# Two rows of scores in one burst, one shared bank for keys, queries and outputs, and a new order of steps in a fused attention, experts and gated-layer kernel

## The chip, the cores and the metric

The kernel runs on one core of a Trainium2 chip. The metric is the device time of one execution in microseconds (us), lower is better. One launch holds the whole computation.

## The reference, cut to what matters

Three layers follow one another, all in float32. The attention has 4 batches of 12 heads with 448 positions and a head width of 64:

```python
scores = scale * np.matmul(q_n, k_n.transpose(0, 1, 3, 2))   # q_n, k_n: rms-normed
scores = scores - np.max(scores, axis=-1, keepdims=True)
attn = np.exp(scores)
attn = attn / (np.sum(attn, axis=-1, keepdims=True) + 1e-09)
return np.matmul(attn, v).astype(np.float32)
```

Its output, 1792 tokens of width 768, goes through 8 experts, one per token:

```python
expert_idx = np.argmax(logits, axis=1)
...
    h = np.maximum(x[mask] @ w1[e], 0.0)
    out[mask] = gate_w[mask, None] * (h @ w2[e])
```

and then through a gated layer: `(gate * val @ w_out)` with `gate = 1 / (1 + exp(-(x @ w_gate)))` and `val = x @ w_val`.

## The kernel before, in words

**Tiling.** The 48 heads are worked through as 24 pairs (G = 2). The 448 query positions of a head are R = 4 "rows" of P = 112 positions. For one row of a pair, `scores` (L338) issues six products of 448 columns: three steps (high times high, high times low, low times high) for each of the two heads. A head takes only 64 of TensorE's 128 rows, so the two heads of a step use the two halves of the array. The result of a head and a row fills one PSUM bank. `peaks` (L351, VectorE) takes the maximum, `exps` (L359, ScalarE) the exponential, and with it the bank is free. `turn_p` (L382, TensorE) transposes 112 columns of all four rows into a bank, `high_p` (L391, ScalarE) and `low_p` (L401, VectorE) split it into a rounded and a rest part, and `values` (L411, TensorE) multiplies both with the values, two products each. After four of them `copy_o` (L425, ScalarE) moves the result to memory, `outputs` (L432, TensorE, eight products) turns it back to positions, and `weigh` (L441, VectorE) divides by the sums. Keys and queries of the next pair come by `turn_k` and `turn_q` (transposes, L313 and L327), `high_k` and `copy_q` (ScalarE, L316 and L330) and `low_k` (VectorE, L320); TensorE turns what `scale_k`, `scale_q`, `high_q` and `low_q` on GpSimd and ScalarE have prepared. `turn_q` is done twice per pair, for the high and for the low part.

**Banks.** PSUM has eight banks here, in four pools: `pss` with 3 (scores), `pst` with 2 (turned probabilities), `psx` with 2 (turned keys and queries, outputs, ranks, and later the turned tokens of the experts) and `psv` with 1 (values). A pool hands its banks out in turn, and whoever gets a bank waits until its last reader is done.

**Order.** Every step of the attention stage is put into one list with a place (a number; one row of a pair is 1, so a pair is 8), and the list is sorted by place (`todo`, L645 to L778). Each engine runs its own instructions in the order in which the sorted list issues them, so a step that waits holds up all that stands behind it on its engine. `WITHIN` (L122) gives the places of a pair's steps relative to its start, `PLACE` (L115) those of the preparation and the routing, `FIRST`, `SECOND` and `EARLY` (L135, L121 and L145) those of the first pairs, and `LT` (L113) moves the last batch's routing. At the end of each batch the routing of its tokens runs beside the attention of the next: `sum_squares` on ScalarE, `choice`, `norms`, `ranks` (three small products into a `psx` bank, L570), `places` and `gates` on VectorE and GpSimd, and `send`, an indirect DMA from GpSimd.

**Experts.** `experts` (L1179) goes through the experts, expert 0 in `first_expert`, then e = 1 to 7 in the loop at L1280. Its second half is a loop over o, six blocks of 128 output columns. At each o, `window_turn(e + 1, o)` (L1198) transposes one block of the next expert's tokens into a `psx` bank, and `high_low` (L1162) reads it, first on ScalarE, then on VectorE. Then come the products of block o, the copy of their result, and `advance` (L1396), the splitting of weights, also on ScalarE and VectorE. From expert 5 on the outputs are taken in pairs (`paired`, L1027): both products of o = 0 and o = 1 are issued at o = 0, none at o = 1, so that the `window_turn` of o = 2 follows directly on that of o = 1:

```python
                if e + 1 < E:
                    window_turn(e + 1, o)
...
                if o == 0 or not paired(e):
                    outs = [result_ps(e) for i in range(2 if paired(e) else 1)]
...
                elif o > 1:
```

**Banks after the attention.** `gemm_ps` (L1034) takes `pss` and `pst` in turn, `either_ps` (L1041) goes through the list `BANKS` (L1039).

## Time and profile before

| | us |
|---|---|
| median of 3 runs | 1170.42 (1170.27 to 1172.71) |
| the profiled execution, its own time | 1169.98 |
| its span, first to last instruction | 1168.3 |
| TensorE products busy in the span | 1135.9 (97%) |
| TensorE weight loads busy | 1020.8 (87%) |
| VectorE busy | 848.0 (73%) |
| ScalarE busy | 568.4 (49%) |
| GpSimd busy | 304.1 (26%) |

How to read it: the span is that of the profiled execution; what lies around it is 1.7 us. PE is TensorE's products, PEld its weight loads, DVE is VectorE, ACT ScalarE, POOL GpSimd. Products are pipelined and their ends are modelled, so the start of one to the start of the next says what a group of products takes, not the length of one. The attention stage ends some 355 us after the span's start, the experts take it to about 650 us, and the gated layer follows.

### The profile page before, as it was taken

Reading aid. Unit: us, or ns where it says so; the run is one execution under the profiler, and the core shown is the slowest. Engines: PE = TensorE matmul, PEld = TensorE weight load, DVE = VectorE, ACT = ScalarE, POOL = GpSimd, SP = SyncE. Lnnn points to the kernel's source line nnn. Section 1 sums busy time; section 2 is a strip of 40 time slices with the busy share of each in tenths; the row PEclk is TensorE's granted clock in tenths of the full one; section 3 lists DMA queues with packets and bytes.
Section 4 is the critical chain, followed back from the end, with each engine's and each line's share of the span. In section 5 each row is a group of like instructions: output and inputs, shape, how many; then the busy total and the mean of one; then the engine's idle time right before and its main releaser. Section 6 shows DMA issues by size and latency. Waiting matters only on the chain.

```text
span 1168.3 us, 19626 instructions
## 1 busy us (share of the span) xinstructions
PE 1135.9 (97%) x7294; PEld 1020.8 (87%) x7295; DVE 848.0 (73%) x1615; ACT 568.4 (49%) x1281; POOL 304.1 (26%) x490
## 2 busy tenths in 40 slices
PE   4999999999999999999999999999999999999996
PEld 2777777777779999999999999999999999999996
DVE  5898899898873155566677968878888868336663
ACT  6789988989872153565666512122211212332220
POOL 5765768778731000000000000000000000021132
PEclk9999999999999999999999999999999999999998
DMA  4414813221235354566767134443444433832031
GB/s 110 127 33 123 259 49 95 49 49 49 73 127 178 110 176 157 180 218 198 224 214 216 55 109 135 153 146 122 152 132 136 132 125 107 345 133 85 27 129 55
DMA packets 97944, 154.55 MB, mean 132 GB/s; under 512 B 4891, under 2 KB 82459, under 8 KB 96947
## 3 DMA queue, kind: packets, MB, share of 16 engines
q1 hardware_dynamic: 91119, 125.69, 34.9%
q0 software_dynamic: 6432, 27.53, 6.3%
q8 instruction: 58, 0.95, 0.3%
q14 instruction: 43, 0.35, 0.1%
q10 hardware_dynamic: 292, 0.03, 0.0%
HBM read 117.84 MB, written 35.39 MB: 131 GB/s over the span
## 4 chain that ended last, share of the span: by engine, by line
PE 63%; issue 3%; POOL 1%; DMA 1%; POOLq 0%
PE psg L1170 42%; PE pso L1170 8%; PE psg L1174 5%; PE psg L1177 2%; PE psg L898 2%; POOL out_dram L797 1%; PE psg L894 1%; PE psw L1205 1%; DMA wout<-wod 1%; PE psw L865 0%; POOL dummy L804 0%; PE pso L1148 0%; POOLq L1817 0%; POOLq L797 0%
## 5 line engine op out<-in xcount | busy, mean ns | idle before, releaser
L1170 PE MATMUL psg<-xs,w 128*128 128x448 f32 x1728 | 351.3, 365 | 0.0
L1170 PEld LDWEIGHTS psg<-xs,w 128*128 128x128 f32 x1728 | 323.9, 188 | 27.1
L1465 POOL DMA_DIRECT2D wod<-so x42 | 22.8, 542 | 601.7 <-DVE hA L1607 352.1
L1170 PE MATMUL pso<-wout,hs 128*128 128x384 f32 x882 | 153.4, 335 | 0.4 <-DMA wout<-wod 0.4
L1170 PEld LDWEIGHTS pso<-wout,hs 128*128 128x128 f32 x882 | 153.0, 188 | 0.7 <-issue 0.6
L1021 DVE TENSOR_TENSOR whl<-raw,whl 128x768 fp32r<-128x768 f32 (+1 forms) x98 | 105.1, 1072 | 60.2 <-ACT whl L1017 60.0
L353 DVE TENSOR_REDUCE nm<-pss 112x1 f32<-112x448 f32 x192 | 116.6, 618 | 26.2 <-PE pss L346 25.4
L406 DVE TENSOR_TENSOR pl<-pst,ph 112x448 fp32r<-112x448 f32 x192 | 115.7, 616 | 17.7 <-ACT ph L393 15.9
L369 ACT ACTIVATE pn<-pss,nm 112x448 f32<-112x448 f32 x184 | 119.2, 648 | 6.7 <-DVE nm L353 6.4
L393 ACT CAST ph<-pst 112x448 fp32r<-112x448 f32 x192 | 101.7, 539 | 21.2 <-PE pst L386 18.5
L386 PE MATMUL pst<-ident,pn 112*112 112x112 f32 x768 | 107.2, 267 | 2.4 <-DVE pl L406 2.3
L386 PEld LDWEIGHTS pst<-ident,pn 112*112 112x112 f32 x768 | 79.0, 136 | 29.1 <-DVE pl L406 12.3
L346 PE MATMUL pss<-kh,qt 64*112 64x448 f32 x384 | 86.8, 425 | 4.1 <-ACT pn L369 3.0
L1017 ACT CAST whl<-raw 128x768 fp32r<-128x768 f32 (+1 forms) x98 | 90.7, 926 | 0.0
L420 PE MATMUL psv<-ph,vt 112*128 112x448 f32 x192 | 82.5, 430 | 0.0
L1443 ACT CAST w<-cva 128x384 fp32r<-128x384 f32 x48 | 24.7, 515 | 109.5 <-DVE cva L1427 109.5
L1170 PE MATMUL psg<-hhl,whl 128*128 128x288 f32 (+3 forms) x576 | 75.1, 287 | 0.0
L346 PEld LDWEIGHTS pss<-kh,qt 64*112 64x112 f32 x384 | 38.0, 179 | 39.4 <-ACT pn L369 13.0
L1170 PEld LDWEIGHTS psg<-hhl,whl 128*128 128x128 f32 x576 | 70.9, 189 | 0.1
L420 PE MATMUL psv<-pl,vt 112*128 112x448 f32 x192 | 70.6, 368 | 0.0
L1170 PE MATMUL psg<-xhl,whl 128*128 128x288 f32 (+3 forms) x576 | 69.8, 282 | 0.0
L1170 PEld LDWEIGHTS psg<-xhl,whl 128*128 128x128 f32 x576 | 69.2, 188 | 0.0
(287 smaller groups left out, 1913.0 us busy)
## 6 DMA issues: line engine op xcount, KB each, us to landing
raw<-in_moe_w_dram SPq DMA_DIRECT2D x28, 768.0 KB, 4.5
raw<-in_moe_w_dram SPq DMA_DIRECT2D x21, 1024.0 KB, 5.5
wod<-so POOLq DMA_DIRECT2D x42, 384.0 KB, 2.6
wout<-wod SPq DMA_DIRECT2D x7, 2304.0 KB, 9.7
raw<-in_moe_w_gate_dram SPq DMA_DIRECT2D x24, 384.0 KB, 3.3
raw<-in_moe_w_val_dram SPq DMA_DIRECT2D x24, 384.0 KB, 3.2
raw<-in_moe_w_out_dram SPq DMA_DIRECT2D x24, 384.0 KB, 3.1
xs<-zero SPq DMA_DIRECT2D x8, 960.0 KB, 8.9
```

Source lines behind the costliest of these rows:

```text
L346: nc.tensor.matmul(sc[g * G + i, r][:P, :S], lhsT=qt[a][rows, r * P : (r + 1) * P], rhs=kk[rows], start=(step == 0), stop=(step == 2),)
L353: nc.vector.tensor_reduce(out=nm, in_=sc[n, r][:P, :S], axis=AX.X, op=ALU.max, negate=True)
L369: nc.scalar.activation(out=pn[n][:, r], in_=sc.pop((n, r))[:P, :S], func=AF.Exp, bias=sc.pop((n, r, "m")), scale=scale(0, 0, n, 1)[:, r] i ...
L386: nc.tensor.transpose(ps[:P, r * P : (r + 1) * P], p[:, r, c * P : (c + 1) * P], ident[:P, :P])
L393: nc.scalar.copy(out=ph, in_=pt[n, c][0][:P, :S])
L406: nc.vector.tensor_tensor(out=pl, in0=ps[:P, :S], in1=ph.bitcast(F32), op=ALU.subtract)
L420: nc.tensor.matmul(ps[:, :S], lhsT=lhs, rhs=p, start=(c == 0 and i == 0), stop=(c == R - 1 and i == len(parts) - 1),)
L1017: nc.scalar.copy(out=splits[p][:, 0, cs], in_=raws[p][:, cs])
L1021: nc.vector.tensor_tensor(out=w[:, 1, cs], in0=raws[p][:, cs], in1=w.bitcast(F32)[:, 0, cs], op=ALU.subtract)
L1170: nc.tensor.matmul(ps, lhsT=lhs[:, a], rhs=rhs[:, b], start=first and i == 0, stop=last and i == 2)
L1174: nc.tensor.matmul(ps.rearrange("p (a n) -> p a n", n=n), lhsT=lhs[:, 0], rhs=rhs, start=first, stop=False)
L1443: nc.scalar.copy(out=hi, in_=af)
```

## The change

The pool of the scores gets four banks in place of three, and `psx` one in place of two. `WITHIN` has new places for all steps of a pair: rows 0 and 1 of the scores stand at -0.572 and -0.176 with no other TensorE step between them (before: -0.572 and 1.615), the row 0 of the second head is taken before that of the first by `peaks` and `exps`, and the last step, `weigh`, stands at 16.314 in place of 18.308. The first pair puts its rows 0, 1 and 3 into `pss` and row 2 into `pst`. The first steps of pair 1 (`SECOND`), the expert embedding (`emb_norm`, `emb_turn`), `scale_k`, `ranks` and `guard`, the routing of the third batch and the two `soon_turn` steps get new places, and `BANKS` names the new pools.

```diff
@@ -57,9 +57,9 @@
     ZP = 80
 
     const = ctx.enter_context(tc.tile_pool(name="const", bufs=1))
-    pss = ctx.enter_context(tc.tile_pool(name="pss", bufs=3, space=PSUM))
+    pss = ctx.enter_context(tc.tile_pool(name="pss", bufs=4, space=PSUM))
     pst = ctx.enter_context(tc.tile_pool(name="pst", bufs=2, space=PSUM))
-    psx = ctx.enter_context(tc.tile_pool(name="psx", bufs=2, space=PSUM))
+    psx = ctx.enter_context(tc.tile_pool(name="psx", bufs=1, space=PSUM))
     psv = ctx.enter_context(tc.tile_pool(name="psv", bufs=1, space=PSUM))
     ident = const.tile([128, 128], F32, name="ident")
     gsc = const.tile([128, 1], F32, name="gsc")
@@ -110,27 +110,27 @@
         nc.gpsimd.tensor_tensor(out=y, in0=y, in1=t, op=ALU.mult)
         yield
 
-    LT = 5.65
+    LT = 3.12
     LAG = 2
     PLACE = dict(
-        eng_q=0, eng_o=0, eng_g=2, load=-49.957, squares=-40, reduces=(-36.19, -32.81), stats=-21.36, scale_k=-14.5,
+        eng_q=0, eng_o=0, eng_g=2, load=-49.957, squares=-40, reduces=(-36.19, -32.81), stats=-21.36, scale_k=-12,
         scale_q=-14.633, high_q=-9.584, high_v=-8.369, low_q=-8.938, low_v=-2.302, invert=4.094,
-        sum_squares=17.264, choice=16.838, norms=24.5, ranks=26.5, gate_x=45.151, 
-        constants=20.3, emb_norm=5.5, emb_step=0.342, emb_turn=13.9, guard=0.264, first_v=-13.224,
+        sum_squares=17.264, choice=16.838, norms=24.5, ranks=30.1, gate_x=45.151, 
+        constants=20.3, emb_norm=4.2, emb_step=0.342, emb_turn=12.45, guard=-0.094, first_v=-13.224,
     )
-    SECOND = (1.6, 2.05, 2.08, 2.0, 2.2, 2.6, 2.65)
+    SECOND = (1.6, 1.65, 1.7, 2.0, 2.2, 2.6, 2.65)
     WITHIN = dict(
-        scores=(-0.572, 1.615, 2.25, 5.231),
-        peaks=((0.255, 1.824, 3.115, 5.933), (0.911, 2.287, 3.427, 6.855)),
-        exps=((0.823, 2.193, 3.708, 6.762), (1.963, 3.066, 5.079, 8.014)),
-        turn_p=((7.635, 9.146, 9.689, 9.918), (10.936, 12.292, 13.427, 14.745)),
-        high_p=((8.335, 9.242, 10.211, 11.042), (12.183, 12.534, 13.773, 14.823)),
-        low_p=((8.731, 9.684, 10.634, 11.12), (12.399, 12.7, 15.294, 15.981)),
-        values=((9.938, 11.282, 12.388, 12.506), (15.258, 16.119, 16.355, 17.251)),
-        copy_o=(13.423, 17.361),
-        outputs=(14.912, 17.815),
-        weigh=(16.279, 18.308),
-        turns=(-8.966, -8.258, -5.914, -4.138, -2.464, -5.426, -4.615),
+        scores=(-0.572, -0.176, 2.978, 4.353),
+        peaks=((0.215, 1.745, 3.616, 4.422), (-0.018, 1.183, 3.741, 5.718)),
+        exps=((0.844, 3.402, 4.627, 5.165), (0.09, 2.649, 5.773, 6.627)),
+        turn_p=((6.369, 7.081, 7.946, 8.276), (10.506, 11.275, 12.497, 12.638)),
+        high_p=((6.447, 7.105, 8.015, 9.096), (10.924, 11.457, 13.121, 13.447)),
+        low_p=((6.912, 7.602, 8.891, 10.516), (11.379, 11.858, 13.435, 13.45)),
+        values=((8.097, 9.159, 10.603, 11.488), (12.851, 13.275, 14.735, 15.408)),
+        copy_o=(12.342, 15.98),
+        outputs=(12.557, 16.013),
+        weigh=(13.243, 16.314),
+        turns=(-6.544, -6.319, -5.061, -3.83, -3.563, -1.983, -1.974),
     )
     FIRST = dict(
         scores=(-0.572, -0.5, 0.25, 1.0),
@@ -149,7 +149,7 @@
         [11.83, 17.498, 21.845, 19.911, 21.838, 25.022, 23.388, 37.052],
         [10.35, None, 25.853, 28.819, 32.85, 36.887, 33.927, 44.019],
         [22.084, 27.843, 31.491, 30.206, 36.193, 40.512, 37.891, 53.712],
-        [23.384, None, 45.6, 44.05, 48.686, 53.754, 49.7, 54.01],
+        [23.384, None, 47.751, 44.05, 48.686, 53.754, 51.087, 54.01],
     ]
 
     def attention(ctx2, rp, after):
@@ -338,7 +338,7 @@
         def scores(g, r):
             kh, kl, *qt = [qkT[g, part] for part in ("h", "l", 0, 1)]
             for i in range(G):
-                pool, tag = (pss, "s") if g or r % 2 == 0 else (pst, "t")
+                pool, tag = (pss, "s") if g or r != 2 else (pst, "t")
                 sc[g * G + i, r] = pool.tile([128, 512], F32, tag=tag, name="pss")
             for step, (a, kk) in enumerate(((0, kh), (0, kl), (1, kh))):
                 for i in range(G):
@@ -360,7 +360,7 @@
             g, j = divmod(n, G)
             if r == 0:
                 pn[n] = wk.tile([P, R, S], F32, tag="pn", name="pn", bufs=4)
-            if n % G == 0 and r == 0:
+            if g not in sums:
                 sums[g] = sm.tile([P, G, R], F32, tag="sums", name="sums", bufs=4)
             if n < G:
                 nc.scalar.activation(
@@ -715,18 +715,18 @@
             t0 = h0 + H * R
             if b == B - 2:
                 for r in range(R):
-                    at(t0 + 11.95 + 1 * r, sum_squares, b, r, 0, 0, H)
-                at(t0 + 11.25, add_logits, b, H)
-                chain(t0 + 11.65, 0.5, choice(b, H))
-                chain(t0 + 15.65, 0.5, norms(b))
-                at(t0 + 17.1, ranks, b)
-                chain(t0 + 18.0, 0.5, places(b))
-                chain(t0 + 18.45, 0.5, provisional(rp))
-                chain(t0 + 22.15, 0.5, gates(b))
+                    at(t0 + 9.42 + 1 * r, sum_squares, b, r, 0, 0, H)
+                at(t0 + 8.72, add_logits, b, H)
+                chain(t0 + 9.12, 0.5, choice(b, H))
+                chain(t0 + 13.12, 0.5, norms(b))
+                at(t0 + 14.57, ranks, b)
+                chain(t0 + 15.47, 0.5, places(b))
+                chain(t0 + 15.92, 0.5, provisional(rp))
+                chain(t0 + 19.62, 0.5, gates(b))
                 for r in range(R):
-                    at(t0 + 25.15 + r, gate_x, b, r, nc.gpsimd)
-                    at(t0 + 26.15 + r, send, b, r)
-                at(t0 + 30.65, soon_rows, rp)
+                    at(t0 + 22.62 + r, gate_x, b, r, nc.gpsimd)
+                    at(t0 + 23.62 + r, send, b, r)
+                at(t0 + 28.12, soon_rows, rp)
             elif slow:
                 for r in range(R):
                     at(t0 + PLACE["sum_squares"] + 1.7 * r, sum_squares, b, r, 0, 0, H)
@@ -757,8 +757,8 @@
                     at(t0 + 0.3 + 0.01 * r, gate_x, b, r, *((nc.vector, nc.scalar), (nc.scalar,), (nc.vector,), (nc.scalar,))[r])
                     at(t0 + 0.3 + 0.01 * r, send, b, r)
                 for i in range(2):
-                    at(t0 - 8.8 + 2 * i, soon_turn, rp, i)
-                    at(t0 - 7.8 + 2 * i, soon_copy, i)
+                    at(t0 - 10.32 + 2.4 * i, soon_turn, rp, i)
+                    at(t0 - 9.32 + 2.4 * i, soon_copy, i)
                 hidden = soon_hidden()
                 for place, n in ((-0.4, 2), (0.16, 9), (0.17, 29), (1.2, 99)):
                     at(t0 + place, steps_of, hidden, n)
@@ -1036,7 +1036,7 @@
         pool, tag = ((pss, "s"), (pst, "t"))[gemm_n[0] % 2]
         return pool.tile([128, 512], F32, tag=tag, name="psg")
 
-    BANKS = [{"s": (pss, "s"), "t": (pst, "t"), "x": (psx, "x"), "v": (psv, "v")}[name] for name in "stxstxsv"]
+    BANKS = [{"s": (pss, "s"), "t": (pst, "t"), "x": (psx, "x"), "v": (psv, "v")}[name] for name in "stsxstsv"]
 
     def either_ps():
         gemm_n[0] += 1
```

## Rows read from the trace of the kernel before

**Rows 1.** Table by stretches: us, busy time of PE, PEld, DVE, ACT, POOL.

```profile
50.00:330.00 280.00, 276.88 (x2122) 213.15 (x2120) 249.24 (x496) 253.80 (x673) 199.93 (x316) 1.00 0.33 97
400.00:1150.00 750.00, 749.64 (x4480) 715.83 (x4481) 533.81 (x955) 257.95 (x471) 54.83 (x90) 1.00 0.46 153
```

**Rows 2.** Timeline of TensorE, first row of scores of four pairs: start, length.

```profile
47.91 0.46 PE L346 MATMUL pss<-kh,qt 64*112 64x448 f32 x2
...
155.41 0.46 PE L346 MATMUL pss<-kh,qt 64*112 64x448 f32 x2
...
168.27 0.46 PE L346 MATMUL pss<-kh,qt 64*112 64x448 f32 x2
...
327.29 0.46 PE L346 MATMUL pss<-kh,qt 64*112 64x448 f32 x2
```

**Rows 3.** Timeline of TensorE around one burst of scores in a quiet pair.

```profile
180.83 0.37 PE L420 MATMUL psv<-pl,vt 112*128 112x448 f32 x1
181.12 0.46 PE L346 MATMUL pss<-kh,qt 64*112 64x448 f32 x2
...
181.92 0.59 PE L386 MATMUL pst<-ident,pn 112*112 112x112 f32 x4
182.28 0.45 PE L420 MATMUL psv<-ph,vt 112*128 112x448 f32 x1
182.57 0.36 PE L420 MATMUL psv<-pl,vt 112*128 112x448 f32 x1
182.76 0.36 PE L420 MATMUL psv<-ph,vt 112*128 112x448 f32 x1
...
183.17 0.55 PE L386 MATMUL pst<-ident,pn 112*112 112x112 f32 x4
183.48 0.45 PE L420 MATMUL psv<-ph,vt 112*128 112x448 f32 x1
```

**Rows 4.** Timeline of TensorE, first pair: rows 0 and 1 follow each other.

```profile
12.24 0.95 PE L346 MATMUL pss<-kh,qt 64*112 64x448 f32 x4
12.99 0.57 PE L346 MATMUL pss<-kl,qt 64*112 64x448 f32 x2
```

**Rows 5.** Timeline of TensorE: keys of pair 2, before the scores of pair 1.

```profile
28.82 1.01 PE L308 MATMUL psk<-ident,ks 112*128 112x112 f32 x4 [2.77 <-POOL ks L259]
```

**Rows 6.** Groups of instructions on ScalarE, 80 to 320 us: the copy of the queries.

```profile
L296 ACT CAST qt<-psq 128x448 fp32r<-128x448 f32 x36 | 19.9, 553 | 7.1 <-PE psq L308 7.1
```

**Rows 7.** Timelines of VectorE and TensorE: a reader ends, a bank is taken again.

```profile
334.57 0.61 DVE L406 TENSOR_TENSOR pl<-pst,ph 112x448 fp32r<-112x448 f32 x1
...
335.33 0.56 PE L386 MATMUL pst<-ident,pn 112*112 112x112 f32 x4 [0.39 <-DVE pl L406]
```

**Rows 8.** Timelines, experts 5 and 6: two turns at once, and the first one's reader.

```profile
582.04 0.54 PE L1205 MATMUL psw<-ident,xw 128*128 128x128 f32 x4
...
584.43 0.38 DVE L1165 TENSOR_TENSOR xhl<-psw,xhl 128x216 fp32r<-128x216 f32 x1
...
613.56 0.94 PE L1205 MATMUL psw<-ident,xw 128*128 128x128 f32 x4
...
615.97 0.35 DVE L1165 TENSOR_TENSOR xhl<-psw,xhl 128x192 fp32r<-128x192 f32 x1
```

**Rows 9.** Timelines, experts 3 and 4: a reader of turned tokens, the next turn.

```profile
512.31 0.40 DVE L1165 TENSOR_TENSOR xhl<-psw,xhl 128x240 fp32r<-128x240 f32 x1
512.57 0.37 PE L1205 MATMUL psw<-ident,xw 128*128 128x128 f32 x2
...
515.59 0.37 PE L1205 MATMUL psw<-ident,xw 128*128 128x128 f32 x2
515.79 0.40 DVE L1165 TENSOR_TENSOR xhl<-psw,xhl 128x240 fp32r<-128x240 f32 x1
...
546.41 0.39 DVE L1165 TENSOR_TENSOR xhl<-psw,xhl 128x232 fp32r<-128x232 f32 x1
546.65 0.36 PE L1205 MATMUL psw<-ident,xw 128*128 128x128 f32 x2
```

## The prediction

> **What bounds the kernel now.** I read the table by stretches first, to find the engine that sets the pace. TensorE has products in flight for 276.9 of 280 us of the attention and for 749.6 of 750 us from the experts on, while VectorE is busy for 249.2 and 533.8 [rows 1]. So time goes only where TensorE gets less work or waits less, and a wait that is added to TensorE after the attention has nothing behind it that would take it up.
>
> Busy includes modelled ends, so I went to the timeline of TensorE and took starts. A quiet pair takes 168.27 - 155.41 = 12.86 us from its first scores to the next pair's [rows 2]. From pair 2 to pair 23 there are 21 such steps, in 327.29 - 47.91 = 279.38 us; 21 x 12.86 is 270.06, so some 9.3 us are waits and the routing's own products.
>
> **The change part by part.** *Fewer bursts.* Around one burst [rows 3] the last product of values before it starts at 180.83, the burst at 181.12, the transposes after it at 181.92 and the values after those at 182.28: 1.45 us. The same work without a change of shape: one product of values is 0.19 (182.57 to 182.76), three steps of scores are as wide and take 0.20 each, and four transposes 0.31 (183.17 to 183.48), 1.10 together. So a burst costs 0.35 us beside its products: 0.10 before it, 0.20 in it, 0.05 behind it. In the first pair, at half the pace, rows 0 and 1 already follow each other, and the block of four products over the seam is 0.95 long against 0.57 for the two behind it, which is 0.38, one step: no gap lies at the seam [rows 4]. Merging two bursts of a pair thus saves 0.35. The new order has one more place where values follow transposes or outputs (7 groups in a pair, 6 before), and the first product after such a change takes 0.29 against 0.19 [rows 3]: 0.10 back. Net 0.25 for each of 23 pairs: **-5.7 us**. Bounds: 0 (the second row waits for its banks) and 0.35 x 23 = -8.0.
>
> The Trainium skill, "TensorEngine Tiling (Array Packing)", section Tiling Modes, says that a change of tiling mode drains TensorE; "TensorE: Matmul & The Clock Gate" puts the drain at some 128 cycles, which I estimate as 0.05 us, twice per burst. By these pages of the Trainium skill a merge would save 0.1, the pair nothing, and the sum would be 1177.8. The row has 0.35, and I go by the row.
>
> *Start.* Before, the scores of pair 1 stand behind the turn of pair 2's keys, which waits 2.77 us for GpSimd [rows 5]. The new order turns those keys after both first rows of pair 1, and puts two transposes of pair 0 ahead of them. What is late next is the copy of pair 1's queries on ScalarE, since the one bank now passes keys, high queries and low queries one by one. I take **-2.0**; bounds 0 and -2.8.
>
> *One bank, in a quiet pair.* It is used five times per pair: outputs, keys, high queries, outputs, low queries. The tightest place is the second outputs: TensorE has the high queries' turn, a burst and four transposes in front of it (some 0.4 + 0.9 + 0.4 = 1.7 us after the last values). ScalarE must do `copy_o` and `copy_q` in that time, about 0.55 each [rows 6]; with 0.2 until the products' end is seen and 0.15 from a reader's end to the next product (335.33 - 334.57 - 0.61) [rows 7] that is 1.45. It fits by a quarter of a us: 0, covered by that burst. Without the cover it is the first rival.
>
> *Ranks.* `ranks` now stands right behind the low queries' turn (batches 0 and 1), or one block of transposes behind it (batch 2), in the same bank, so TensorE waits for `copy_q`: 0.2 + 0.55 + 0.15 = 0.9, 0.9 and 0.6: **+2.4**; behind it stand the next pair's transposes. Bounds 0 (TensorE is waiting at the end of a batch anyway) and 5.
>
> *One bank, in the experts.* This the list of attention steps does not show. In experts 5 and 6 the turns of o = 1 and o = 2 are issued together [rows 8]. With one bank the second waits for the first one's last reader, the subtraction on VectorE. Expert 5: the first half of the turns ends at 582.04 + 0.27 = 582.31, the reader at 584.43 + 0.38 = 584.81; with 0.15 the wait is 2.65. Expert 6: 613.56 + 0.47 = 614.03, 615.97 + 0.35 = 616.32, 2.44. Together 5.1. These readers are late because ScalarE copies the products of o = 0 and splits weights in front of them; nothing hides that, TensorE is full on both sides [rows 1]. In expert 3 the reader ends at 512.71, the next turn starts at 512.57: 0.29 with the 0.15; its next reader ends at 516.19, the turn stood at 515.59, now at 515.88: 0.46 more. The three later turns I estimate at half a us in all, since a wait moves the turn but not what its reader stands behind: 1.3. In expert 4, 546.80 against 546.65 gives 0.3, about every second turn, 0.6 [rows 9]. Sum 5.1 + 1.3 + 0.6 = **+7.0**. Bounds: 5.1 alone, and 8.6 if no turn gets anything back.
>
> *Edits at nothing.* `BANKS` still comes back to a bank after eight groups and `gemm_ps` has one more; `sums` is only claimed by whichever head comes first. `scale_k` goes 2.5 places later on GpSimd, behind its neighbours there, and the turn of the keys 2.4 places later with it. `soon_rows` and the scatters of batch 2 are 2.5 places earlier on SP and GpSimd, and SP's load of rows still lies two pairs before its first use. `LT` moves the last routing forward with the last `weigh`, so what follows it keeps its order. The cover of each is TensorE's own work; if it is gone, each costs under 1 us.
>
> **Sum.** -5.7 - 2.0 + 2.4 + 7.0 = +1.7, on the execution's own 1169.98 us (span 1168.3): 1171.7. The median of the runs shown is 0.44 above that execution: **1172.1**. A measurement tells about 0.2% here, 2.3 us, from no change.
>
> **The rivals.** *The shared bank becomes the wait in every pair (slower).* At the second outputs there is a quarter of a us of slack. It decides as soon as ScalarE is later than that by the time it reaches `copy_q`, as it will be in pairs where it also casts queries and values, 0.55 or more each [rows 6]. 0.55 - 0.25 = 0.3 per pair, 23 pairs: +7, 1179. For it: ScalarE is busy for 253.8 of 280 us [rows 1]. Against: in the new order it stands idle after each first burst, and can catch up there. Chance 0.12.
>
> *The second row of the burst still pays (slower).* If what a burst loses inside and behind (0.25) comes with each row's first weights, only the 0.10 in front of it is saved, and the new change to values takes that back: the 5.7 are gone, 1177.8. Against it stands the seam without a gap [rows 4]. The two pages of the Trainium skill named above would go with so small a saving. Chance 0.12.
>
> *The waits go too (faster).* The new order is shallower by two places, and its slack is spread anew. If half of the 9.3 us of waits between the pairs goes, the time is 1172.1 - 4.6 = 1167.5, and 1165 if the start gains all and the ranks cost nothing. For it: a walk along the new list finds every TensorE step of a quiet pair with its input ready. Against: the waits lie at the ends of batches, where ScalarE and VectorE have the routing's work on top, and a shorter pair leaves them less room. Chance 0.31.
>
> *The change doesn't do what it says* would be a second row that waits in the middle of the burst for the banks of the previous pair's last exponentials; this is the bound 0 of the first term, also 1178, and I count it with the second rival.
>
> **How the numbers follow.** The forecast, a little slower or no change that can be told, has 0.45; its own range is 1169.5 to 1175. Of it 0.28 fall within 0.2% (up to 1172.8), 0.15 are slower, 0.02 faster. The two slower rivals add 0.24 to slower; of the faster one 0.22 are beyond 0.2% and 0.09 within. So faster 0.24, same 0.37, slower 0.39. The range goes from 1166.5 to 1177.5, which leaves out about 1 in 10 on either side.
>
> **What would show it.** Right: in a quiet pair two rows of scores 0.6 apart, three bursts, and some 12.6 us per pair; the table by stretches with idle TensorE time near the 5th and 6th expert; TensorE's turn of tokens in these waiting 2.4 to 2.7 us for the subtraction; small waits of the same kind in experts 3 and 4; scores of pair 1 ahead of pair 2's keys. Wrong: no wait of TensorE behind a turn of tokens, or one that is made up before the end; quiet pairs over 12.8 us, with outputs or queries waiting for ScalarE; quiet pairs under 12.5, or an attention that ends more than 9 us earlier.

## The result and the profile after

The kernel after takes 1182.57 us (median of 4 runs, 1180.99 to 1185.88), beside 1170.35 us for the kernel before in the same measurement: a ratio of 1.0103 (95% interval 1.0087 to 1.0118), 12.2 us slower. The forecast was 1172.1 with a range up to 1177.5. The profiled execution of after is its longest, 1185.88 us with a span of 1184.2, 15.9 us above the span of before; the ledger below is made with that pair, and where another execution of the same code differs, it is said.

The page of the kernel after: the span, the busy times, and the granted clock of TensorE in 40 slices.

```profile
span 1184.2 us, 19538 instructions
PE 1138.4 (96%) x7294; PEld 1032.1 (87%) x7295; DVE 842.0 (71%) x1615; ACT 563.9 (48%) x1281; POOL 304.3 (26%) x490
PEclk8799999999999999999998999999999999999999
```

TensorE's products are busy for 2.5 us more than before, and idle for 13.4 us more. The clock line has lower digits: 8 and 7 in the first two slices and a later 8, where before every slice but the last had 9. The later one is a stretch of expert 6 (below). For the start the two lines can't be compared. The record of before reads 1.00 there, but its products run at half pace until about 41 us, as the rows say. First before (the table with columns as in [rows 1], and behind POOL's the granted clock, the DMA share and GB/s; then the timeline of TensorE):

```profile
36.00:40.00 4.00, 4.00 (x17) 2.81 (x18) 3.03 (x6) 2.72 (x9) 3.59 (x8) 1.00 0.92 238
```

```profile
39.89 0.95 PE L386 MATMUL pst<-ident,pn 112*112 112x112 f32 x4
...
41.58 0.55 PE L386 MATMUL pst<-ident,pn 112*112 112x112 f32 x4
```

and the timeline of TensorE after:

```profile
42.94 0.99 PE L386 MATMUL pst<-ident,pn 112*112 112x112 f32 x4
...
49.65 0.54 PE L386 MATMUL pst<-ident,pn 112*112 112x112 f32 x4
```

The same four transposes reach the fast pace at about 41 us before. After, they have it from about 32 us on (0.55 at 32.94), lose it at 39.27 and have it again from 49.65.

The table by stretches, answering to [rows 1] (columns as there).

```profile
50.00:330.00 280.00, 271.14 (x2105) 216.52 (x2103) 243.46 (x491) 247.35 (x666) 200.87 (x316) 0.99 0.32 93
400.00:1150.00 750.00, 744.02 (x4417) 707.75 (x4416) 523.01 (x940) 254.50 (x467) 48.10 (x80) 0.99 0.46 152
```

TensorE now has 8.9 idle us in the first stretch (3.1 before) and 6.0 in the second (0.4 before). Where they are, the timeline of TensorE of the kernel after says; in brackets the wait before a row and its releaser.

```profile
37.74 0.59 PE L386 MATMUL pst<-ident,pn 112*112 112x112 f32 x4 [1.59 <-DVE pl L406]
...
39.27 0.97 PE L308 MATMUL psq<-ident,qs 112*128 112x112 f32 x4 [0.50 <-DVE kl L323]
...
50.55 0.46 PE L346 MATMUL pss<-kh,qt 64*112 64x448 f32 x2
...
156.24 0.37 PE L575 MATMUL psr<-base,ident 112*112 112x16 f32 x2 [0.93 <-ACT qt L296]
...
158.57 0.46 PE L346 MATMUL pss<-kh,qt 64*112 64x448 f32 x2
...
171.11 0.46 PE L346 MATMUL pss<-kh,qt 64*112 64x448 f32 x2
...
183.79 0.46 PE L346 MATMUL pss<-kh,qt 64*112 64x448 f32 x2
184.08 0.37 PE L346 MATMUL pss<-kl,qt 64*112 64x448 f32 x2
184.29 0.56 PE L346 MATMUL pss<-kh,qt 64*112 64x448 f32 x4
184.69 0.36 PE L346 MATMUL pss<-kl,qt 64*112 64x448 f32 x2
184.89 0.37 PE L346 MATMUL pss<-kh,qt 64*112 64x448 f32 x2
185.19 0.60 PE L386 MATMUL pst<-ident,pn 112*112 112x112 f32 x4
...
196.35 0.46 PE L346 MATMUL pss<-kh,qt 64*112 64x448 f32 x2
...
287.36 0.81 PE L436 MATMUL pso<-fold,ot 128*112 128x72 f32 x6 [1.56 <-ACT qt L296]
...
332.68 0.46 PE L346 MATMUL pss<-kh,qt 64*112 64x448 f32 x2
...
590.99 0.41 PE L1205 MATMUL psw<-ident,xw 128*128 128x128 f32 x2 [2.47 <-DVE xhl L1165]
...
595.13 0.56 PE L1205 MATMUL psw<-ident,xw 128*128 128x128 f32 x2
...
626.76 0.78 PE L1205 MATMUL psw<-ident,xw 128*128 128x128 f32 x2 [2.33 <-DVE xhl L1165]
...
632.18 0.71 PE L1205 MATMUL psw<-ident,xw 128*128 128x128 f32 x2
```

What to see: the two rows of scores in one burst are 0.61 apart (184.69 against 184.08), with no gap at the seam, and a quiet pair takes 196.35 - 183.79 = 12.56 us in place of 12.86. The gain is there. Against it stand the waits through the shared bank: at the ranks for the copied queries (156.24), at outputs (287.36), and at a turn of tokens in experts 5 and 6 (590.99, 626.76); at the start (37.74, 39.27) TensorE waits for VectorE. Behind some of these the products are slow: the next turn of tokens follows 4.14 and 5.42 us later, where 2.80 and 2.96 are enough with two banks (the first run below). The table by stretches of 4 us shows why (columns as in the table of before above).

```profile
40.00:44.00 4.00, 4.00 (x26) 3.17 (x25) 2.92 (x7) 1.19 (x4) 3.92 (x4) 0.50 0.88 195
44.00:48.00 4.00, 4.00 (x20) 3.72 (x20) 2.60 (x6) 2.80 (x7) 1.59 (x2) 0.50 0.00 1
...
588.00:592.00 4.00, 1.53 (x11) 1.25 (x11) 2.99 (x5) 3.08 (x6) 0.00 (x0) 1.00 0.59 195
592.00:596.00 4.00, 4.00 (x18) 3.67 (x17) 0.90 (x3) 0.63 (x2) 0.00 (x0) 0.57 0.58 175
624.00:628.00 4.00, 1.67 (x8) 1.01 (x6) 3.17 (x5) 2.90 (x6) 0.00 (x0) 0.80 0.55 189
628.00:632.00 4.00, 4.00 (x15) 3.79 (x14) 0.39 (x2) 0.00 (x0) 0.00 (x0) 0.50 0.64 197
```

TensorE is granted 0.50 of its clock, the lower level of 1.2 GHz, right behind the wait: 18 and 15 products in 4 us, where the same windows of the first run below, with two banks, have 27 and 29.

**The ledger** (us of the profiled pair, after less before):

| stretch | forecast | measured | from |
|---|---|---|---|
| to the first scores of pair 2 | -2.0 | +2.6 | 50.55 against 47.91 [rows 2] |
| pairs 2 to 23 | -2.85 (bursts -5.25, ranks +2.4) | +2.75 | 282.13 against 279.38 |
| last pair, to the last outputs | -0.5 | -1.4 | 24.16 against 25.60 |
| experts, first to last turn of tokens | +7.0 | +11.7 | 235.25 against 223.58 |
| rest | 0 | +0.3 | |
| sum | +1.7 | +15.9 | |

By the first scores of each pair, the second row divides so: the last two pairs of each of the first two batches take 1.5 us more than before, the two at the end of the third batch 3.1 more, and the other fifteen together 3.4 less, 0.23 each.

### The profile page after: what moved, and what is told of

It is laid out like the page before. It is cut to its first block, busy times and chain, and to the rows that moved or that the text cites. A ratio compares the mean times of both kernels' runs of the same rounds, so it can differ in the third digit from the quotient of the medians.

```text
span 1184.2 us, 19538 instructions
## 1 busy us (share of the span) xinstructions
PE 1138.4 (96%) x7294; PEld 1032.1 (87%) x7295; DVE 842.0 (71%) x1615; ACT 563.9 (48%) x1281; POOL 304.3 (26%) x490
## 4 chain that ended last, share of the span: by engine, by line
PE 61%; issue 3%; POOL 1%; DMA 1%; ACT 1%; DVE 1%; POOLq 0%; ACTq 0%
PE psg L1170 41%; PE pso L1170 8%; PE psg L1174 5%; PE psg L1177 2%; PE psg L898 2%; POOL out_dram L797 1%; PE psg L894 1%; PE psw L1205 1%; DMA wout<-wod 1%; ACT whl L1017 0%; DVE whl L1021 0%; PE psw L865 0%; DVE xhl L1165 0%; POOL dummy L804 0%; PE pso L1148 0%
## 5 line engine op out<-in xcount | busy, mean ns | idle before, releaser
L406 DVE TENSOR_TENSOR pl<-pst,ph 112x448 fp32r<-112x448 f32 x192 | 118.4, 617 | 34.8 <-ACT ph L393 34.2
L393 ACT CAST ph<-pst 112x448 fp32r<-112x448 f32 x192 | 105.5, 549 | 36.1 <-PE pst L386 35.4
L386 PE MATMUL pst<-ident,pn 112*112 112x112 f32 x768 | 112.0, 270 | 6.6 <-DVE pl L406 6.3
L386 PEld LDWEIGHTS pst<-ident,pn 112*112 112x112 f32 x768 | 80.7, 137 | 37.2 <-DVE pl L406 15.6
L353 DVE TENSOR_REDUCE nm<-pss 112x1 f32<-112x448 f32 x192 | 111.3, 609 | 0.6 <-PE pss L346 0.6
L420 PE MATMUL psv<-ph,vt 112*128 112x448 f32 x192 | 85.4, 445 | 0.0
L346 PE MATMUL pss<-kh,qt 64*112 64x448 f32 x384 | 78.1, 411 | 2.7 <-ACT pn L369 2.0
```

What stands on the lines that cost most here:

```text
L346: nc.tensor.matmul(sc[g * G + i, r][:P, :S], lhsT=qt[a][rows, r * P : (r + 1) * P], rhs=kk[rows], start=(step == 0), stop=(step == 2),)
L353: nc.vector.tensor_reduce(out=nm, in_=sc[n, r][:P, :S], axis=AX.X, op=ALU.max, negate=True)
L386: nc.tensor.transpose(ps[:P, r * P : (r + 1) * P], p[:, r, c * P : (c + 1) * P], ident[:P, :P])
L393: nc.scalar.copy(out=ph, in_=pt[n, c][0][:P, :S])
L406: nc.vector.tensor_tensor(out=pl, in0=ps[:P, :S], in1=ph.bitcast(F32), op=ALU.subtract)
L420: nc.tensor.matmul(ps[:, :S], lhsT=lhs, rhs=p, start=(c == 0 and i == 0), stop=(c == R - 1 and i == len(parts) - 1),)
```

## The experiments

Theory: (1) the merged burst gains as forecast; (2) the one bank makes waits, in the experts above all, but also at the ends of batches; (3) behind some of these waits TensorE falls to its lower clock, which raises their price. Rivals: the new order is slow in itself; the waits cost their length and no more.

All ratios are to the kernel before, measured beside each kernel; its medians there are 1169.88 to 1170.35, so a difference between two of the kernels below can be off by half a us for that alone. The number to follow for the experts is the time from the first turn of tokens in the experts to the last one, in each kernel's profile, because no attention is in it: 223.58 us before, 235.25 after.

### One bank or two in the experts

**The kernel after, with two banks for these turns again.**

```diff
-            ps = psx.tile([128, 512], F32, tag="x", name="psw")
+            pool, tag = (psv, "v") if e > 2 and c % 2 else (psx, "x")
+            ps = pool.tile([128, 512], F32, tag=tag, name="psw")
```

> The kernel after, with the expert turns after the third expert going through two banks in turn again (every other turn uses the bank of the values). Theory (one bank makes a wait of 2.3 to 2.5 us in experts 5 and 6, and the granted clock falls to its lower level after it): the whole loss of the experts comes back, 11.7 us by the two profiles, so about 1170.7 us, and the granted clock around 590 and 628 us stays near 1. Rival (only the waits and nothing else are the bank's; the rest of the loss has another source in the new order): 7 us come back, about 1175.6 us. Attention unchanged within 0.5 us in both.

Measured: 1173.54 us, ratio 1.0030 (1.0019 to 1.0042), between the two forecasts. The stretch of the experts takes 223.76 us, that is the time of before, and the granted clock is 1.00 all through it; the turn of o = 3 follows that of o = 2 in 2.80 us in expert 5 and 2.96 in expert 6. So all of the 11.7 us of the profile are the bank's. The medians differ by 9.0. That other executions of after pay less than 11.7 would explain it, and is likely, since the profiled one is the longest; no profile of them shows it.

**The kernel before, with one bank for these turns:** the mirror image.

```diff
-            ps = psx.tile([128, 512], F32, tag="x", name="psw")
+            pool, tag = (psv, "v") if e > 2 else (psx, "x")
+            ps = pool.tile([128, 512], F32, tag=tag, name="psw")
```

> The kernel before, with the expert turns after the third expert going through one bank only; attention is that of before. Theory (wait plus lower granted clock behind it): slower than before by about 11.7 us, some 1182 us, with waits of 2.3 to 2.6 us in experts 5 and 6 and the granted clock well under 1 in the 4 us after each. Rival (the waits alone): slower by 7 us, some 1177.4 us, granted clock near 1.

Measured: 1179.57 us, 1.0077 (1.0060 to 1.0094), between the two forecasts; the profiled execution, 1181.20, is near the theory's. Attention is that of before (first turn of tokens at 399.50 against 399.33); the experts' stretch takes 235.23 us, as in the kernel after. The new order has no part in this loss. Its timeline of TensorE and its table by stretches, expert 5:

```profile
587.11 0.41 PE L1206 MATMUL psw<-ident,xw 128*128 128x128 f32 x2 [2.47 <-DVE xhl L1165]
...
591.14 0.56 PE L1206 MATMUL psw<-ident,xw 128*128 128x128 f32 x2
```

```profile
588.00:592.00 4.00, 4.00 (x18) 3.67 (x17) 1.01 (x3) 0.62 (x2) 0.00 (x0) 0.57 0.57 173
```

**The same, with TensorE at work in the wait.** The kernel above, with eight pairs of products that nobody reads right ahead of each of the two turns that wait; they are left out of every result.

```diff
+                if e + 1 < E and paired(e) and o == 2:
+                    fill = psx.tile([128, 512], F32, tag="x", name="fill")[:, : 2 * WIN[e]]
+                    for i in range(8):
+                        mul(e, fill, splits[...][:, :, 0, ...], hh[:, :, 0], True, True)
                 if e + 1 < E:
                     window_turn(e + 1, o)
```

> The kernel before with one bank for the expert turns (measured 1179.57 us, two waits of 2.47 and 2.33 us), and TensorE given eight pairs of products that nobody reads right ahead of each of the two waiting turns, about 2.1 us by the mean product there, so that it works where it waited. Theory (the waits themselves cost about 7 us, and the rest is the granted clock that falls after an idle stretch): the granted clock stays at 1.00 in experts 5 and 6, the last turn of experts 5 and 6 follows the third by some 2.8 to 3.1 us rather than 4.0 and 5.4 us, and the median comes to before plus 7.2, about 1177.3 us, with the fast and the slow executions close together. Rival (the clock falls for another reason, as the load of the products): still 1179.6 us or slower by what the products add.

Measured: 1177.10 us, 1.0057 (1.0044 to 1.0070), as the theory has it and *faster* than without the added products: by 2.5 us, or by 2.3 if each is taken against the before beside it. The two intervals overlap, but none of these 5 runs (1175.51 to 1177.28) reaches the 4 without the products (1178.42 to 1181.20). Timeline of TensorE and table by stretches:

```profile
585.62 0.27 PE L1177 MATMUL fill<-hhl,whl 128*128 128x232 f32 x1
585.75 0.41 PE L1206 MATMUL psw<-ident,xw 128*128 128x128 f32 x2
...
588.62 0.35 PE L1206 MATMUL psw<-ident,xw 128*128 128x128 f32 x2
```

```profile
584.00:588.00 4.00, 4.00 (x27) 3.61 (x26) 3.25 (x5) 1.93 (x5) 0.00 (x0) 1.00 0.33 116
588.00:592.00 4.00, 4.00 (x29) 3.75 (x28) 1.65 (x3) 1.71 (x5) 0.00 (x0) 1.00 0.89 301
```

The turn of tokens comes as late as it did, but the next one follows after 2.87 us, at a clock of 1.00. The stretch takes 230.71 us: before plus 7.1. That is the price of the waits alone, and it is the +7.0 of the prediction; the rest, up to 4.5, is the clock. One profile without a fall could be luck, since a kernel without the added products had none either (the split burst, below); but its stretch took the same time, so the price does not hang on this profile. That the load of the products draws the clock down does not fit, since here it is higher.

The Trainium skill bears on this with two sentences. "TensorE: Matmul & The Clock Gate", section "A second HAM failure mode: psum-queue depth-cycling", tells of a kernel that lost throughput because TensorE idled briefly between groups while it cycled through banks; the trace agrees that idle time comes before the lower clock (0.57 behind 2.47 us of waiting, 1.00 where the same time is filled), though not behind every such wait (the table below). "Perfetto Trace Analysis", section "Optimizing Tensor Performance", wants independent groups to rotate through different banks; here the rotation was worth 7.1 us of waits and up to 4.5 of clock.

**Two ways to shorten the wait with one bank.** First, the third turn behind the products of its own step; then, the second turn ahead of the weight split, so that VectorE reads it earlier.

```diff
+                late = paired(e) and o == 2
-                if e + 1 < E:
+                if e + 1 < E and not late:
                     window_turn(e + 1, o)
...
+                if e + 1 < E and late:
+                    window_turn(e + 1, o)
```

> The kernel after, still with one bank, but for the experts whose products are paired the third turn of the window is issued behind the products of its own step instead of ahead of them. Theory: the reader of the bank has some 2 us more, so the wait of 2.47 and 2.33 us in experts 5 and 6 is gone and with it the fall of the clock: 9.5 us back (4.26 + 5.23), about 1173.1 us. Rival (loss is the waits alone, clock falls for another reason): 4.8 us back, about 1177.8 us.

Measured: 1178.83 us, 1.0062 (1.0041 to 1.0082): the forecast of the theory was missed, because the waits did not go. Timeline of TensorE:

```profile
594.31 0.41 PE L1205 MATMUL psw<-ident,xw 128*128 128x128 f32 x2 [1.32 <-DVE xhl L1165]
...
627.40 0.53 PE L1205 MATMUL psw<-ident,xw 128*128 128x128 f32 x2 [1.07 <-DVE xhl L1165]
```

The turns wait behind the products instead of ahead of them, for 1.32 and 1.07 us. The clock is 1.00 behind both, and the stretch takes 228.48 us, 6.8 less than after. The median gained only 3.7: in its profile the slow products behind the outputs' wait in the attention cost more than in any other run (below), and the runs go from 1173.25 to 1179.82.

```diff
-                if e + 1 < E:
+                if e + 1 < E and not (paired(e) and o == 1):
                     window_turn(e + 1, o)
...
+                if e + 1 < E and paired(e) and o == 0:
+                    window_turn(e + 1, 1)
                 advance(pools, p, (oo > 0))
```

> The kernel after, still with one bank, but for the paired experts the second turn is issued ahead of the weight steps of the first product step, so that VectorE reads the bank ahead of them: the wait shrinks from about 2.4 to about 1.1 us and does not go. It tells what the length of a wait does to the clock. Theory A (the clock holds after a short wait): the wait shrinks by 2.6 us in all and 4.2 to 4.7 us of slow products go: about 6.8 us back, 1175.8 us. Theory B (any wait there drops the clock): 2.7 us back, 1179.9 us.

Measured: 1178.55 us, 1.0074 (1.0057 to 1.0091), between the two. The waits of 2.47 and 2.33 have become two each, 0.85 and 0.50, 0.80 and 0.33; the clock is 1.00 behind all, and the stretch takes 228.78 us, 6.5 less than after, as theory A has it. As a median it is 4.0: the profile of after is an execution with both falls; that its other executions have fewer is likely and not shown.

### The waits in the attention

**The ranks behind the copy of the queries.**

```diff
-        sum_squares=17.264, choice=16.838, norms=24.5, ranks=30.1, gate_x=45.151, 
+        sum_squares=17.264, choice=16.838, norms=24.5, ranks=31.42, gate_x=45.151, 
-                chain(t0 + PLACE["ranks"] + 1.2, 0.5, places(b))
+                chain(t0 + PLACE["ranks"] + 0.19, 0.5, places(b))
```

> The kernel after, with the ranks of a batch placed 1.32 us later, so that the copy of the queries on ScalarE is done before them. Theory (the ranks waited 0.93 and 0.95 us for that copy through the shared bank): 1.8 us faster, 1180.8 us, and no wait over 0.3 us at the ranks. Rival (the path through the end of a batch is set elsewhere, and the wait is taken over by the next product): no change.

Measured: 1176.32 us, 1.0057 (1.0035 to 1.0078), 6.2 us faster than after, over three times what was expected. In the profile the wait is gone, and the pair at the end of a batch takes 13.88 and 13.87 us in place of 15.10 and 15.12: 2.5 in all, 0.6 more than the two waits. The rest of the 6 us stood in stretches whose code is the same (the third pair's scores at 47.51 rather than 50.55, one fall of the clock in the experts rather than two), so it was put to a test of its own ("less the ranks", below).

**The sums of squares of the third batch spread out.** For 287.36 of the kernel after, the timeline of ScalarE shows what stood ahead of the copy of the queries:

```profile
284.23 0.88 ACT L459 ACTIVATE junk<-xn 112x768 f32<-112x768 f32 x1
...
285.46 0.59 ACT L296 COPY ot<-psv 128x448 f32<-128x448 f32 x1
285.89 0.90 ACT L459 ACTIVATE junk<-xn 112x768 f32<-112x768 f32 x1
...
286.73 0.58 ACT L296 CAST qt<-psq 128x448 fp32r<-128x448 f32 x1
```

```diff
-                    at(t0 + 9.42 + 1 * r, sum_squares, b, r, 0, 0, H)
+                    at(t0 + (9.42, 10.92, 12.7, 14.4)[r], sum_squares, b, r, 0, 0, H)
...
-                chain(t0 + 13.12, 0.5, norms(b))
+                chain(t0 + 15.65, 0.5, norms(b))
```

(and `ranks`, `places`, `provisional`, `gates`, `gate_x`, `send` and `soon_rows` where they stood before the change)

> The kernel after with only the sums of squares of the third batch spread out (and the steps after them where they stood before). Theory: the wait of 1.56 us of the outputs for the copy of the queries goes; from the scores of pair 18 to those of pair 20 it takes 27.7 us (13.8 each) instead of 30.5, and the median falls by 1.5 to 3 us to about 1180 us. Rival (ScalarE is full there whatever the order; the wait comes back at the next step): no change, 1182.6 us.

Measured: 1180.35 us, 1.0077 (1.0062 to 1.0093), at the theory's number, though the interval overlaps that of after. The profile decides: the outputs no longer wait; from the scores of pair 18 to those of pair 20 it takes 26.92 us in place of 30.46. Some comes back: the pair behind takes 15.15 in place of 13.79.

The 1.56 us wait stood at the same place, at the same length within 0.01, in all seven kernels that kept this order, and cost a different amount: the pair of this wait takes 16.67 and 16.68 us in two of them, at a clock of 1.00 throughout, and 17.91, 18.29, 18.29, 18.57 (the split burst, 0.34 longer in every pair) and 20.54 in the others, with the clock at the lower level for part of the next 4 to 10 us. So the fall of the clock is not settled by the wait's length.

**The start.** The reduces of the fourth pair's squares, with their statistics (10.6), are moved out of the way of the last low part of the first head's probabilities.

```diff
-        [7.45, 9.863, 12.14, 11.457, 13.872, 14.464, 17.181, 17.111],
+        [7.45, 10.6, 12.14, 11.457, 13.872, 14.464, 17.181, 17.111],
-                    for place in (ts, *((-0.4, 2.0), (1.9, 1.91), (9.4, 9.6))[g - 1]):
+                    for place in (ts, *((-0.4, 2.0), (1.9, 1.91), (10.53, 10.56))[g - 1]):
```

> The kernel after, with the reduces of the squares of the fourth pair and its statistics placed later, so that the last product's sum of the first pair is not behind them on VectorE and TensorE's wait of 1.59 us at 37.74 us goes. Theory (several waits there make the granted clock fall to its lower level from about 39 to 49 us): without it the first scores of the third pair come some 5 us earlier (45.5 rather than 50.5 us), and the whole is about 5 us faster, 1177.5 us. Rival (the wait costs only its own length, the slow stretch comes anyway): 1.5 us faster, 1181 us, the granted clock of 40 to 48 us still 0.5.

Measured: 1181.83 us, 1.0099 (1.0077 to 1.0120), no gain that can be told. The theory is refuted; the rival's 1181 lies within the interval, but the wait was not saved as it said. Timeline of TensorE:

```profile
37.43 0.60 PE L386 MATMUL pst<-ident,pn 112*112 112x112 f32 x4 [0.40 <-DVE pl L406]
...
40.13 0.60 PE L308 MATMUL psq<-ident,qs 112*128 112x112 f32 x4 [1.69 <-DVE kl L323]
```

The wait has moved: the low part of the keys now stands behind the reduces, and the two waits together are 2.09 us as they were. The granted clock is 0.76 and 0.50 from 40 to 48 us. The third pair's scores are at 50.43.

### The merged burst

```diff
-        scores=(-0.572, -0.176, 2.978, 4.353),
+        scores=(-0.572, -0.04, 2.978, 4.353),
```

> The kernel after, with the second score row placed behind the first row of values again, so that each pair has one burst of 64-row products more, as before. Theory (each merged burst saves about 0.3 us of products): 0.25 to 0.35 us for each of 23 pairs lost, 5.7 to 8 us slower than the kernel after, about 1188.3 to 1190.6 us; a quiet pair takes 12.85 rather than 12.55 us. Rival (the burst gains nothing, the shorter quiet pair comes from another part of the new order): no change, 1182.6 us.

Measured: 1186.48 us, 1.0148 (1.0123 to 1.0173), 3.9 us slower than after by the medians, where 5.7 to 8 were forecast. Pair by pair the profile has the forecast: in the timeline of TensorE the scores of pairs 11 and 13 are 25.92 us apart,

```profile
170.06 0.46 PE L346 MATMUL pss<-kh,qt 64*112 64x448 f32 x2
...
195.98 0.46 PE L346 MATMUL pss<-kh,qt 64*112 64x448 f32 x2
```

against 196.35 - 171.11 = 25.24 in the kernel after: 0.34 for each burst, the 0.35 of the prediction's first step. From pair 2 to pair 23 it is 288.88 against 282.13, 6.75 more. Why the medians show less stays open. In this profile the clock held at 1.00 in experts 5 and 6 behind the same two waits (2.49 and 2.34 us), and their stretch took 230.77 us, the same as with the waits filled; and the third pair's scores were at 47.02.

### All repairs together

The kernel after with two banks for the turns, the late ranks and the spread sums.

> The kernel after with three repairs together: two banks for the expert turns, the ranks behind the copy of the queries, and the four sums of squares of the third batch spread out so that none stands right ahead of the copy on ScalarE for which the outputs waited 1.55 us (with the steps that follow from them at the places they had before). Theory: what is left is the gain of the merged bursts. By the profile of the run with two banks (third pair's scores at 48.8, 282.4 us from there to the last pair's), less 2.5 for the two ranks, 1.6 for the slow products behind the 1.55 us wait and 1.5 for that wait, the attention ends some 3.1 us ahead of before: about 1167 us, faster than both kernels. Rival (the new order is slow in itself, and another wait takes the place of each): 1170 to 1173 us.

Measured: 1167.02 us (9 runs, 1165.90 to 1168.86), 0.9974 (0.9965 to 0.9984): 2.9 us faster than before, 15.6 faster than after, and at the theory's number. The quiet pairs take 12.53 to 12.68 us, the experts 223.77. Timeline of TensorE at the outputs that had waited:

```profile
281.25 0.59 PE L386 MATMUL pst<-ident,pn 112*112 112x112 f32 x4
281.74 1.00 PE L436 MATMUL pso<-fold,ot 128*112 128x72 f32 x8
```

**A second try at the start,** on that version: the same reduces one step later still, behind the low part of the keys (10.95 and 10.96, the statistics at 11.0).

> The same with the reduces of the fourth pair's squares behind the low part of the third pair's keys on VectorE. The earlier try put them between the two steps for which TensorE waits there and so only moved the wait (0.40 in place of 1.59, but 1.69 in place of 0.50). Theory: both waits get short, the granted clock stays up from 39 to 47 us, third pair's scores at about 47 us, 1 to 2 us faster than without it. Rival (a reduce of 1.25 us has no free place there, the next product waits for it): no change.

Measured: 1170.21 us, 0.9994 (0.9985 to 1.0003), 3.2 us slower than without it. The keys still come late, and a third wait joins them: the timeline of TensorE has

```profile
39.34 0.60 PE L308 MATMUL psq<-ident,qs 112*128 112x112 f32 x4 [1.65 <-DVE kl L323]
...
41.73 0.71 PE L346 MATMUL pss<-kh,qt 64*112 64x448 f32 x1 [1.40 <-ACT pn L369]
```

and the clock at 0.50 from 44 to 48 us; the third pair's scores are at 52.11. The new order's start is not mended by this.

**The version with all repairs, less the ranks.**

> The version with the three repairs, less the one at the ranks: these stand ahead of the copy of the queries' reader again in the first two batches. Moving the ranks alone had brought 6.2 us where the two waits of 0.94 us and what follows them take 2.5 us of the profile. Theory (2.5 us are the ranks', the rest was the granted clock of other stretches, which differs between executions): 2.5 us slower than the version with all three, about 1169.5 us. Rival (the ranks' wait costs 6 us, since the rest of the batch is thrown off by it): about 1173 us.

Measured: 1169.34 us (12 runs), 0.9990 (0.9979 to 1.0000): 2.3 us slower than with it. So the ranks are worth 2.3 by the medians and 2.5 by the profiles, and the other 3.7 us of the run in which they alone were moved are not theirs. Its profile had fewer falls of the clock; whether its other runs had is not known.

### What the runs say together

The stretch of the experts in the profiles (first to last turn of tokens); a fall is counted where the turn of o = 3 follows that of o = 2 (expert 5 or 6) after more than 4.0 us in place of 2.8 to 3.0:

| kernel | us | over before | falls |
|---|---|---|---|
| before | 223.58 | | 0 |
| two banks (four kernels) | 223.76 or 223.77 | +0.2 | 0 |
| one bank, waits filled | 230.71 | +7.1 | 0 |
| one bank, burst split | 230.77 | +7.2 | 0 |
| one bank, ranks moved; start moved | 232.38; 232.34 | +8.8 | 1 |
| one bank, sums spread | 234.12 | +10.5 | 2 |
| one bank, in the order of before; after | 235.23; 235.25 | +11.7 | 2 |

## Why the prediction was wrong

*Fewer bursts, -5.7: right.* A quiet pair is 0.30 us shorter (forecast 0.25), and splitting the burst again costs 0.34. The rival by which the second row still pays has fallen with it. The saving of 0.1 estimated from two pages of the Trainium skill, "TensorEngine Tiling (Array Packing)", section Tiling Modes, being one, is not borne out either: the trace has 0.34 per burst, and the measurement decides.

*One bank, in the experts, +7.0: the mechanism and the waits right, the price too low.* The waits were forecast at 2.65 and 2.44 and are 2.47 and 2.33, in part because a product follows the end of the bank's reader after 0.06 us (the reader's end at 590.93, the turn at 590.99) and not 0.15; with TensorE kept at work the stretch costs 7.1. What the step lacked is what TensorE does after it has waited: in 8 of 12 such waits it came back at the lower clock. That is up to 4.5 us in the profile, and about 2 in the medians (9.0 and 9.5 for taking the second bank back or away, less 7.1).

*Start, -2.0: this step failed.* It took the one wait that goes [rows 5] and let nothing come in its place; the wait it did name as next, for the copy of pair 1's queries, is not the one that cost. The first scores of pair 1 did come earlier (28.62 against 29.75), but behind them TensorE in the profiled execution waits 1.59 us for VectorE's low probabilities and 0.50 for the low keys, and then runs at 0.50 of the clock until about 49.5 us, while the kernel before, slow until 41 us, stays fast from there. In eight profiles with this start the third pair's scores come between 47.51 and 50.69 us, 49.1 in the mean, so +1.2 against the 47.91 of before, where -2.0 was forecast. VectorE's order around the start was not followed at all. That the waits bring the slow stretch is not shown, since both tries at the start moved them and did not remove them.

*One bank, in a quiet pair, 0: right where the pair is quiet, wrong at the end of the third batch.* The tight place was named, the second outputs with a quarter us of slack, and the cover too; but of the third batch's routing only the scatters and `soon_rows` were followed (under edits at nothing), and not the sums of squares, 0.9 us each on ScalarE, which the change moves right ahead of that copy. The outputs wait 1.56 us, and the clock takes 0 to 3.9 more.

*Ranks, +2.4: right in the first two batches* (0.93 and 0.95 where 0.9 was forecast), too high in the third (0.24 to 0.26 in five other runs, where 0.6 was forecast). With what follows, the first two alone are worth 2.5, so that the sum came out right in part by luck.

*Edits at nothing: not borne out as a group.* In the kernel after, the ends of the first two batches have further waits (0.46 at 134.30, 0.27 at 144.79, and 0.45 and 0.27 at 213.83 and 224.34), and the third batch's has 1.14 at 300.96; in the kernel before, the first two batches' ends have none of 0.2 or more. The one of 1.14 is gone in the runs in which the third batch's routing is moved back and its sums are spread. No run tells whether the others come from these edits or from the new places of the pairs' steps. The cover named was TensorE's own work; there is none at an end of a batch, since TensorE is the engine that waits.

The rival by which the bank becomes a wait in every pair is near in time (1179) but wrong in kind: quiet pairs do not wait. The one by which the waits go too is the reverse of what happened; by repairing them its time could be reached, 1167.02 against its 1167.5, which is a coincidence of two sums and no proof of its terms (and its 1165 comes to 1164.3 by the terms that it names). What stays open: why the last pair is 0.9 us shorter than forecast, which of the start's steps would have to move, and what decides whether the clock falls behind a wait.

## What to carry to other kernels

Where TensorE is full, a bank taken from a pool must be paid for in every stage that uses the pool, so look for the stage whose readers are late; and price a wait of TensorE by its length and, as a second case, by slow products behind it. A wait that can't be removed can be filled with products that nobody reads; filling the two of some 2.4 us made the kernel 2.3 to 2.5 us faster. When a hand-made order is moved as a whole, follow the slow ends (start, ends of batches) on the engines that feed TensorE, and not only the repeating pair.

## What the runs showed of the hardware

- Of 12 waits of 2.33 to 2.49 us in a TensorE that was full before and after, 8 were followed by the lower clock. Of 7 waits of 1.55 to 1.56 us at one place, 5 were; of 11 of 1.55 to 1.57 us at another (70.90 in the kernel after), one was. Of six waits of 0.33 to 1.32 us in the experts, none. The same code has both outcomes, so it is a risk to be priced and not a certainty.
- In experts 5 and 6 one fall costs 1.6 us and two cost 3.4 to 4.5 (the table above, less the 7.2 without any); in the attention one costs 1.2 to 3.9 behind a wait of 1.55, that is up to two and a half times the wait itself.
- Products that are not needed made a kernel 2.3 to 2.5 us faster (1179.57 to 1177.10) by filling two waits.
- The record of the granted clock can read 1.00 over products at half pace: in the kernel before until about 41 us, four transposes at 0.95 us in place of 0.55.
